# A DeltaNet and hard-swish MLP kernel on one core: X of steps 2 and 3 from products, the first steps in a new order, and products of the identity on TensorE

## The chip, the core and the metric

The kernel runs on one core of one Trainium2 chip. A core has TensorE (matrix products, PE in the profile; its weight loads are PEld), VectorE (DVE), ScalarE (ACT), GpSimd (POOL) and SyncE (SP), which here only issues DMAs. Each engine works through its own instructions in order; semaphores tie them together. TensorE's products land in PSUM, everything else lives in SBUF. The metric is the time of one execution on the device in microseconds; lower is better.

## The reference

Two computations follow each other. The first is a delta rule over 768 tokens, for 4 batches and 8 heads, head size 48:

```python
for t in range(S):
    y[:, :, t] = q_t @ state
    v_old = state^T k_t
    state = state + beta_t * outer(k_t, v_t - v_old)
```

with k normalised to length 1 first. Its output, 3072 tokens by 384, is x of the second:

```python
h = x @ w_in                         # 384 x 2048
g = h * clip(h + 3, 0, 6) / 6
out = g @ w_out                      # 2048 x 384
```

The arrays q, k, v and beta come in float32, the two weights in float64.

## The kernel before

**Steps.** The 768 tokens are cut into 24 steps of 32 tokens; a step holds the four batches beside each other in the 128 partitions. Within a step the sequential rule is a triangular system, so each step needs X, minus the inverse of a 32x32 unit triangular matrix for each head and batch. What is carried from step to step is `state`.

**Preparation of a step** (`prep`, L378 to L455). GpSimd normalises k into `kb` (L383), makes the masked beta `mb` (L391, two operations) and later `bkb` (L438); TensorE transposes k and q (`pt`, L409), ScalarE copies them out (`KQ`, L412), TensorE forms the score products (`sc`, L425), and VectorE multiplies them with `mb` into `LB` (L434). The norms come from `norms` (L337): square and sum (`sq`, `ss`), a square root on ScalarE, and small operations on VectorE.

**X in two ways.** For steps 0 and 1, `product` (L457) gets X by products of 32x32 blocks: six groups of products on TensorE (`pi`, L485), each followed by transposes and additions on VectorE or copies on ScalarE (L495 to L543), in strict alternation. For later steps, `inverse` (L551) takes a group of four steps at once: the matrices go out to DRAM and come back with one system to a partition (`A`), 30 rounds of a multiplication and a subtraction on VectorE solve them (L566, L571), and X goes out to DRAM and back into `LB`. The groups before are steps 0 and 1, then fours (2 to 5, 6 to 9, ...), and a last two.

**The chain of a step** (`chain`, L601): `ks` on TensorE from `state` (L622), `R` and `y` on VectorE (L635), `pz` (L643) with X, `Z` on ScalarE (L685), `su` (L710) and `py` on TensorE, the new `state` on VectorE (L726), and `yt`, the transposed output (L699), which feeds the MLP.

**The MLP** takes blocks of two steps. `up` (L750): 16 units of three products `ph` (L760), each with an activation on ScalarE (L765) and one operation `g` on VectorE (L772). `down` (L788) has plain products for the first two blocks (`po`, L795); from the third on `down_by_seven` (L836) uses seven half-size products (L856) with additions on VectorE.

**Weights.** Each of 16 pieces of 768 KB of float64 is loaded raw; `scales` (L288) builds its power of two in five activations of ScalarE, `convert` (L306) makes the float32 value in three operations of VectorE.

**What sets the order.** [...] The string `ORDER` (L22) lists by hand which generator advances next, until the chain of step 5 is done: `p` preparation, `x` product, `i` inverse, `h` chain, `n` norms, `a` scales, `c` convert, `u` one MLP unit, `g` its late VectorE part, and `k`, `q`, `v`, `w` loads. From step 6 on a loop with a fixed plan does it (L1043), 15 MLP units to a step. Loads go to SP's queue; some of the first k and q loads, and the DMAs of the first inverse, go to ScalarE's queue.

Of the kernel before, what the change touches and what calls it, by code (L numbers as in the profile page):

```python
# [22 lines left out]
n0*8 n1 p0 n1 p0 n1 p0 q*2 p0 q p1 q p1 n1 p0 p1 a n1 a*2 p0 q*2 a*2 c a q p1 x0 n1*2 a n1*3 a  # L23
p2*2 x0 q c k2 p2 a p1 p3 x1 c p3*2 p2 a x1*2 p2 p4 p1 a*2 x1 k2*2 p3 p2 a*3 p3 k2 p5 x0 c*2
k2*3 p3 x0 c a*4 x0 k2 c*3 p4 p5 k2*2 x1 k2 x0 p4 c*2 p5 p4 p5 p4*2 p5 x1*2 k2 x0 p5 a x1 a i1 c
x0 x1 a x0 c x1 k2 x1 x0*2 k2 c i1 v k2 i1 x1 i1 x0 i1*2 a i1*2 x0 q i1*3 a i1 h0*2 i1*3 q i1*3
h0 i1*3 v i1 x1 i1 q i1 h0 i1*3 a i1*2 a h1 a*2 h1 i1*2 h0 i1 h1 q h1 i1 c i1 v h1*2 v i1 h1 k2
i1*5 v i1 v i1 v c w v i1 a c a*2 i1 a i1 c i1 v q i1 a v*2 i1 v a c i1*4 w i1*2 h1 n2 i1*4 a
i1*3 a i1 h2 i1*2 c a i1 a i1 n2 a c*2 u a g c n2 a c u a n2 g u n2*3 a n2 q c a g n2*2 a c a p6
h2 u h2 c p6 a w p6 u q*2 a v g q*2 a h2 p6 c q*2 v u p7 a q p6 a q p7 p6 v p8 c g q h2 v h2 a c  # L30
w a p7 a k3 h3 u k3 p8 u a h2*2 k3 c g k3 g c h3 c h3 p8 a u k3 a k3 p7 u g q p8 u q w k3 p7 h3
a p9 p8 c a p9 k4 g p9 k4 p7 a*2 g u k3 k4 c k4 h3 a h3 p9 c w k3 k4 k3 a p9 g*2 h3 a c h4 k4 k3
u a h3 c g k4 h4 k3 c w u p8 k3*2 g k3 h4 k3 q a n3 a c n3 c a n3 u q u g u h4 a g p9 a c k4 h4
c a n3 a u a w k4 i2 w*2 a*2 u n3 a h4 v h5 h4 c a u c g n3 c n3*2 g v*2 u h4 n3 u v n3 u c p10
q a*2 q g k4 v q i2 p11 k4 u k4*4 p10 i2*2 q*2 i2*2 k4 u v i2*2 h5 v g h5 i2 a i2 q i2 p10 u h5
u v i2*2 q u i2*2 c i2 p10 g u i2 p10 i2*4 p11 p10 h5*2 q u q h5 p11 g u p11 i2 u i2*2 p12 i2 g
i2*2 p11*2 u i2*2 u i2*3 g i2 u*2 g i2 u*2 g u g u*2 g u i2*6 u*4 h5
# [4 lines left out]
def kernel(  # L42
# [34 lines left out]
    CB = 2  # L77
    TB = CB * P
    assert N % CB == 0 and CB <= GS

# [6 lines left out]
    NPC, NPM = 2, 4  # L87
    psC = ctx.enter_context(tc.tile_pool(name="psC", bufs=NPC, space=PSUM))
    psM = ctx.enter_context(tc.tile_pool(name="psM", bufs=NPM, space=PSUM))
# [43 lines left out]
    def load_k(t, eng=nc.sync):  # L133

        g, i = group(t)
        if i == 0:
            needs(*(("kb", first(g - 2) + j) for j in range(size(g - 2) if g >= 2 else 0)))
            kfs[g] = stage.tile([P, GS, H, D], FP32, name="kf", bufs=2)
        for b in range(B):
            eng.dma_start(out=kfs[g][rows(b), i], in_=tokens(k, b, t))  # L140
            if b == B - 1:
                past.add(("k", t))
            yield

    def load_q(t, eng=nc.sync):
        if t < N:
            if t >= NQB:
                needs(("qT", t - NQB))
            for b in range(B):
                eng.dma_start(out=qbufs[t % NQB][rows(b), :, 0:D], in_=tokens(q, b, t))  # L150
                if b == B - 1:
                    past.add(("q", t))
                yield
# [3 lines left out]
    def load_v(t):  # L157
        if t < N:
            if t >= NVF:
                needs(("R", t - NVF))  # L160
            vfs[t] = stage.tile([P, H, D], FP32, name="vf", bufs=NVF)
            for b in range(B):
                nc.sync.dma_start(out=vfs[t][rows(b)], in_=tokens(v, b, t))
                if b == B - 1:
                    past.add(("v", t))
                yield
# [61 lines left out]
    places = const.tile([128, 6], FP32, name="places")  # L228
    for i, value in enumerate((1152 - 7.5 / 16, -1600.0, -448.0, -704.0, 704.0 * 128, 1e-30)):
        nc.vector.memset(places[:, i : i + 1], value)  # L230
    powers = (
        (ACTF.Relu, 1.0 / 16), (ACTF.Abs, 1.0), (ACTF.Relu, 1.0), (ACTF.Abs, 1.0),
        (ACTF.Relu, -128.0),
    )
# [53 lines left out]
    def scales():  # L288

        for i in range(NW):  # L290
# [5 lines left out]
            d, z = raws[i], like(es[i % 2], i)  # L296
            for n, (func, scale) in enumerate(powers):
                nc.scalar.activation(  # L298
                    out=z, in_=z if n else d.bitcast(I16)[:, :, :, 3], func=func,
                    bias=places[:, n : n + 1], scale=scale,  # L300
                )
                if n == len(powers) - 1:
                    past.add(("scale", i))
                yield
# [32 lines left out]
    def norms(g, i0, n):  # L337
# [17 lines left out]
        nc.scalar.activation(out=root[:], in_=ss[:], func=ACTF.Sqrt, bias=places[:, 5:6])  # L355
# [14 lines left out]
        for i in range(n):  # L370
            invs[first(g) + i0 + i] = inv[:, i, :]
        yield
# [5 lines left out]
    def prep(t, dma):  # L378
# [3 lines left out]
        needs(*([("bkb", t - NKB)] if t >= NKB else []))  # L382
        nc.gpsimd.tensor_tensor(  # L383
# [17 lines left out]
        for j, src in enumerate((kb, qb)):  # L401
# [3 lines left out]
            ring("pm", NPM, ("pt", t, j))  # L405
            read(("pt", t, j))
            pt = psM.tile([128, NP, P], FP32, name="pt", tag="pm")
# [38 lines left out]
        if g > 0:  # L446
# [3 lines left out]
            dma.dma_start(  # L450
# [6 lines left out]
    def product(t, pool):  # L457
# [6 lines left out]
        needs(("bkb", t))  # L464
# [3 lines left out]
        VY = pool.tile([P, 2, H * C], FP32, name="VY", bufs=CB)  # L468
        V, Y = VY[:, 0, :], VY[:, 1, :]
        T = pool.tile([P, H * C], FP32, name="VT", bufs=CB)  # L470
        F = pool.tile([P, H * C], FP32, name="F", bufs=CB)
# [3 lines left out]
        def times(rhs):  # L475
# [3 lines left out]
            ring("pm", NPM, key)  # L479
            keys.append(key)  # L480
            ps = psM.tile([P, 2, H * C], FP32, name="pi", tag="pm")
# [69 lines left out]
    def inverse(g, dma, back):  # L551
# [5 lines left out]
        dma.dma_start(  # L557
# [4 lines left out]
        for j in range(1, C - 1):  # L562
# [3 lines left out]
            nc.vector.tensor_tensor(  # L566
# [4 lines left out]
            nc.vector.tensor_tensor(  # L571
# [3 lines left out]
        nc.vector.memset(A.rearrange("p c i -> p (c i)")[:, 0 : C * C : C + 1], -1.0)  # L575
        back.dma_start(
# [4 lines left out]
        for i in range(size(g)):  # L581
            yield
            LBv = LBs[first(g) + i][:].rearrange("p e a j w -> p (e a) j w")
            back.dma_start(out=LBv[:, :, 0, :], in_=x_dram[g][i].rearrange("h p c -> p h c"))
# [16 lines left out]
    def chain(t):  # L601
# [78 lines left out]
        ring("pm", NPM, ("pz", t))  # L680
        read(("pz", t))
        pz = psM.tile([P, 512], FP32, name="pz", tag="pm")
# [6 lines left out]
        def seam():  # L689

            blk, cc = divmod(t, CB)
# [3 lines left out]
            ring("pm", NPM, ("yt", t))  # L695
            read(("yt", t))
            pt = psM.tile([128, NKT, P], FP32, name="yt", tag="pm")
# [21 lines left out]
        ring("pm", NPM, ("py", t))  # L719
        py = psM.tile([P, 512], FP32, name="py", tag="pm")  # L720
# [29 lines left out]
    def up(blk):  # L750

        needs(*(("seam", blk * CB + i) for i in range(CB)))
        xT = xTs[blk]
        for f in range(NFC):
            needs(("w", f * 128 // WP))
            settle(2)
            ring("pm", NPM, ("ph", blk, f))
            ph = psM.tile([128, TB], FP32, name="ph", tag="pm")
# [23 lines left out]
    def to_dram(t, o):  # L782
        for b in range(B):
            r0 = b * S + t * C
            eng = nc.scalar if t >= N - CB and b % 2 else nc.sync
            eng.dma_start(out=out[r0 : r0 + C, :], in_=o[rows(b ^ 1)])

    def down(blk, c, f0):  # L788

        needs(("w", NWI + f0 // WF))  # L790
        if f0 == 0:
            ring("pm", NPM, ("po", blk, c))
            pos[c] = psM.tile([128, DM], FP32, name="po", tag="pm")
# [5 lines left out]
        if f0 + WF == NFC:  # L799
            if c == 0:  # L800
                pos["o"] = mlp[0].tile([128, CB, DM], FP32, name="o", bufs=1)
# [3 lines left out]
            to_dram(blk * CB + c, o)  # L805
# [14 lines left out]
    assert 2 * WP * NKT == HF * HM and CB == 2 and HF % 2 == 0  # L820
# [15 lines left out]
    def down_by_seven(blk):  # L836
# [8 lines left out]
        o = mlp[0].tile([128, CB, DM], FP32, name="o", bufs=1)  # L845
        u = mlp[0].tile([128, HM], FP32, name="u", bufs=1)[:]
        C11, C12, C21, C22 = (o[:, c, m : m + HM] for c in range(CB) for m in (0, HM))
        ps = {}

        def product(n, a, b, half):  # L850

            if half == 0:
                ring("pm", NPM, ("po", blk, "by", n))
                ps[n] = psM.tile([128, HM], FP32, name="po", tag="pm")
# [60 lines left out]
        to_dram(blk * CB + 1, o[:, 1])  # L915
        product(3, A12, B22, 1)
        add(C12, u, ps[3][:])
        to_dram(blk * CB, o[:, 0])
        yield

    def mlp_units():
# [4 lines left out]
        for f in range(0, NFC, WF):  # L926
            for c in range(CB):
# [6 lines left out]
        for blk in range(1, N // CB):  # L934
            if blk < FIRST:
                settle()
                for c in range(CB):
# [5 lines left out]
            if blk + 1 < N // CB:  # L943
# [21 lines left out]
    LA = CB + GS  # L965
# [6 lines left out]

    def prep_of(t):
        return made(("p", t), lambda: prep(t, nc.scalar if t < LA else nc.sync), t < N)

# [3 lines left out]
    def norms_of(g):  # L979
        return made(("n", g), lambda: norms(g, 0, size(g)), g < NG)  # L980

    def inverse_of(g):
        return made(("i", g), lambda: inverse(g, nc.scalar if g == 1 else nc.sync, nc.sync), g < NG)

    def keys_of(g):
        return made(
            ("k", g), lambda: chained(*(load_k(first(g) + i) for i in range(size(g)))), g < NG
        )

    def pieces(i):  # L990
        for i in range(i, NW):
            load_w(i)
# [5 lines left out]
    gens["w"] = pieces(NWI)  # L998

    with tc.manual_schedule():  # L1000
        with tc.tile_pool(name="early", bufs=2) as early:
            for t in range(LA):
                drain(load_k(t, nc.scalar if t % 2 else nc.sync))
                if t == 1:
                    drain(load_q(0))
                    drain(load_q(1, nc.scalar))
            for t in range(CB, NQB):
                drain(load_q(t))
            for i in range(3):
                load_w(i, early if i < 2 else stage)  # L1010
            for t in range(CB):
                drain(load_v(t))
# [99 lines left out]
```

## Time and profile before

| | us |
|---|---|
| median of 3 runs | 724.28 (723.74 to 726.2) |
| the profiled execution's own time | 726.81 |
| its span, first to last instruction | 725.1 |
| TensorE busy | 656.7 (91%) |
| VectorE busy | 454.9 (63%) |
| ScalarE busy | 247.3 (34%) |
| GpSimd busy | 89.5 (12%) |

The profile page cuts the span into 40 slices of 18.1 us; a digit is the busy share of an engine in tenths. PEclk is the clock granted to TensorE, in tenths of full speed. In the answers by window, the columns are the window, its length, and for PE, PEld, DVE, ACT and POOL the busy time and the number of instructions; then the clock, the share of the DMA engines and GB/s. In the timeline a line is start, duration, engine, line of the program and tile; the bracket is the idle time before it and what ended that. In the groups, after the bar, come busy time and the mean of one in ns, then idle time before the group.

A product in float32 is two records in the trace.

### The profile page before, as it was taken

To read this page: it belongs to the slowest core of one execution; us is meant where nothing else is said; L and a number is where in the kernel's file an instruction comes from. 1 tells how busy PE (TensorE), PEld (TensorE's weight loads), DVE (VectorE), ACT (ScalarE), POOL (GpSimd) and SP (SyncE) were. 2 spreads that over 40 slices of the span, in tenths; PEclk is the share of its full clock that TensorE was granted. 3 is DMA by queue.
4 is the path that set the end of the run, shared out by engine and by line. 5 is a ranking of instruction groups with operands and counts; after the bars stand their busy time and mean duration, and the time that the engine had idled before them with its cause. 6 is when DMAs were issued, how large, how long until landed. Compare 5 with 4: busy or idle time off the path is not lost.

```text
span 725.1 us, 25019 instructions
## 1 busy us (share of the span) xinstructions
PE 656.7 (91%) x10984; PEld 571.9 (79%) x10984; DVE 454.9 (63%) x1209; ACT 247.3 (34%) x467; POOL 89.5 (12%) x128
## 2 busy tenths in 40 slices
PE   0666839798979999999999999999999999999997
PEld 0455627666756789889889899898898898989997
DVE  6556996488583379665489464598444894533343
ACT  1763688593130331331322322322313213222130
POOL 3640024004031101041110031000000000000000
PEclk9966569899999999999999999999999999999999
DMA  7954437472042312421410411212302001000000
GB/s 135 298 119 89 112 91 176 90 183 37 8 96 48 75 32 42 90 36 26 96 32 15 98 33 31 52 21 60 53 2 50 13 16 39 2 24 1 23 1 22
DMA packets 135853, 44.72 MB, mean 62 GB/s; under 512 B 126112, under 2 KB 129184, under 8 KB 135744
## 3 DMA queue, kind: packets, MB, share of 16 engines
q1 hardware_dynamic: 126832, 40.99, 25.4%
q10 hardware_dynamic: 8912, 2.13, 1.5%
q8 instruction: 86, 1.41, 0.8%
q14 instruction: 23, 0.19, 0.1%
HBM read 32.60 MB, written 10.49 MB: 59 GB/s over the span
## 4 chain that ended last, share of the span: by engine, by line
PE 78%; issue 7%; DVE 5%; DMA 4%; POOL 2%; ACT 2%; SPq 1%; POOLq 0%; DVEq 0%
PE ph L760 31%; PE po L856 26%; PE po L795 3%; PE pz L643 3%; PE ks L622 3%; PE su L710 3%; PE py L643 3%; PE pt L409 3%; PE sc L425 2%; DMA kf<-in_k_dram 2%; DMA spare<-in_moe_w_in_dram 1%; PE pi L485 1%; ACT spare L298 1%; DMA vf<-in_v_dram 1%; PE yt L699 1%
## 5 line engine op out<-in xcount | busy, mean ns | idle before, releaser
L760 PE MATMUL ph<-xT,w_in 128*128 128x256 f32 x1152 | 269.6, 386 | 2.6 <-issue 2.3
L760 PEld LDWEIGHTS ph<-xT,w_in 128*128 128x128 f32 x1152 | 216.4, 193 | 34.7 <-issue 3.0
L765 ACT ACTIVATE t<-ph,halves 128x256 f32<-128x256 f32 x192 | 90.8, 474 | 207.3 <-PE ph L760 204.6
L772 DVE SCALAR_TENSOR_TENSOR g<-t,ph 128x256 f32<-128x256 f32 x192 | 79.8, 418 | 120.5 <-ACT t L765 120.3
L856 PE MATMUL po<-w_out,g 128*128 128x192 f32 x640 | 111.9, 327 | 0.0
L856 PEld LDWEIGHTS po<-w_out,g 128*128 128x128 f32 x640 | 104.2, 190 | 0.5
L856 PE MATMUL po<-spare,g 128*128 128x192 f32 x480 | 87.2, 330 | 0.0
L856 PEld LDWEIGHTS po<-spare,g 128*128 128x128 f32 x480 | 78.0, 190 | 1.2
L298 ACT ACTIVATE spare<-spare,places 128x768 uint16<-128x768 uint16 (+1 forms) x74 | 69.2, 940 | 7.7 <-DVE w_in L327 3.3
L566 DVE TENSOR_TENSOR pr<-A 128x30 f32<-128x30 f32 (+19 forms) x180 | 62.8, 349 | 4.1
L571 DVE TENSOR_TENSOR A<-A,pr 128x30 f32<-128x30 f32 (+19 forms) x180 | 61.9, 344 | 4.1
L842 DVE TENSOR_TENSOR g<-g 128x256 f32<-128x256 f32 x160 | 60.4, 428 | 3.7 <-PE po L856 3.5
L409 PE MATMUL pt<-ident,kb 128*128 128x128 f32 x96 | 18.3, 326 | 32.8 <-POOL kb L383 32.8
L795 PE MATMUL po<-w_out,g 128*128 128x384 f32 x128 | 45.4, 494 | 0.0
L383 POOL TENSOR_TENSOR kb<-kf,inv 128x384 f32<-128x384 f32 x24 | 23.5, 979 | 176.0 <-DVE inv L369 73.0
L412 ACT ACTIVATE KQ<-pt 128x512 f32<-128x512 f32 x48 | 28.2, 594 | 47.4 <-PE pt L409 47.4
L409 PEld LDWEIGHTS pt<-ident,kb 128*128 128x128 f32 x96 | 13.8, 167 | 36.0 <-POOL kb L383 33.8
L863 ACT ACTIVATE o<-po 128x192 f32<-128x192 f32 x40 | 13.2, 331 | 82.8 <-PE po L856 79.7
L391 POOL TENSOR_TENSOR mb<-beta_tok,mask 128x256 f32<-128x256 f32 x48 | 33.8, 724 | 56.2 <-DVE LB L434 56.2
L726 DVE TENSOR_TENSOR state<-state,su 128x384 f32<-128x384 f32 x46 | 23.3, 548 | 22.2 <-PE su L710 22.2
L795 PEld LDWEIGHTS po<-w_out,g 128*128 128x128 f32 x128 | 23.5, 192 | 12.9 <-issue 0.5
L635 DVE SCALAR_TENSOR_TENSOR R<-ks,parity,vf 128x192 f32<-128x192 f32 x46 | 16.9, 410 | 26.3 <-PE ks L622 26.2
(97 smaller groups left out, 581.5 us busy)
## 6 DMA issues: line engine op xcount, KB each, us to landing
spare<-in_moe_w_out_dram SPq DMA_DIRECT2D x8, 768.0 KB, 5.4
vf<-in_v_dram SPq DMA_DIRECT2D x96, 48.0 KB, 2.6
qb<-in_q_dram SPq DMA_DIRECT2D x92, 48.0 KB, 2.4
out_dram<-o SPq DMA_DIRECT2D x92, 48.0 KB, 1.6
kf<-in_k_dram SPq DMA_DIRECT2D x84, 48.0 KB, 2.8
w_out<-in_moe_w_in_dram SPq DMA_DIRECT2D x4, 768.0 KB, 9.6
LB<-x_dram SPq DMA_DIRECT2D x22, 128.0 KB, 3.1
x_dram<-A SPq DMA_DIRECT2D x5, 512.0 KB, 2.8
```

Source lines behind the costliest of these rows:

```text
L298: nc.scalar.activation(out=z, in_=z if n else d.bitcast(I16)[:, :, :, 3], func=func, bias=places[:, n : n + 1], scale=scale,)
L391: nc.gpsimd.tensor_tensor(out=mb[:, e], in0=beta_tok[:, t, e:H:2].unsqueeze(2).unsqueeze(3).to_broadcast([P, NP, 2, C]), in1=mask2[:].unsq ...
L409: nc.tensor.transpose(pt[:, p, :], src[:, 2 * p : 2 * p + 2].rearrange("p e w -> p (e w)"), ident[:])
L566: nc.vector.tensor_tensor(out=pv, in0=A[:, j, j + 1 :].unsqueeze(1).to_broadcast([n, j, w]), in1=A[:, 0:j, j].unsqueeze(2).to_broadcast([n ...
L571: nc.vector.tensor_tensor(out=A[:, 0:j, j + 1 :], in0=A[:, 0:j, j + 1 :], in1=pv, op=ALU.subtract)
L643: nc.tensor.matmul(ps[rows(place(b)), D * h : D * h + D], lhsT=m(h)[rows(b)], rhs=z[rows(b), D * h : D * h + D], start=True, stop=True, sk ...
L760: nc.tensor.matmul(ph[:], lhsT=w_in[:, s, f * 128 : (f + 1) * 128], rhs=xT[:, s, :], start=(s == 0), stop=(s == NKT - 1),)
L765: nc.scalar.activation(out=t1[:], in_=ph[:], func=ACTF.Relu, bias=half, scale=1.0 / 6.0)
L772: nc.vector.scalar_tensor_tensor(out=g, in0=t1[:], scalar=1.0, in1=ph[:], op0=ALU.min, op1=ALU.mult)
L795: nc.tensor.matmul(pos[c][:], lhsT=gs[blk, f // 2][:, f % 2, c * P : (c + 1) * P], rhs=w_out[:, f, :], start=(f == 0), stop=(f == NFC - 1),)
L842: nc.vector.tensor_tensor(out=A(f, *out), in0=A(f, *a), in1=A(f, *b), op=op)
L856: nc.tensor.matmul(ps[n][:], lhsT=A(f - f % 2, *a)[:, f % 2], rhs=b[:, f], start=(f == 0), stop=(f == HF - 1),)
```

## The change

- **Groups.** Steps 0 to 3 now form the first group (`CB` 4; a new `BK` = 2 keeps the MLP's blocks). X of steps 2 and 3 also comes from `product`; the buffers are shared with steps 0 and 1, so step 2 follows step 0 and step 3 step 1. The groups with an inverse are 4 to 7, 8 to 11, up to 20 to 23: five in place of six.
- **The first inverse** (steps 4 to 7) runs on GpSimd; the others stay on VectorE.
- **Identity products.** `busy` multiplies the identity with itself into a PSUM tile that nothing reads. The word `z` puts one into TensorE's order; there are 79, all before the first MLP unit.
- **PSUM.** Until the first MLP unit there are three buffers and one for the identity products, after it four as before.
- **Scales** take three activations in place of five.
- **Norms** of steps 0 and 1 are made each by itself, and `kb` of step 0 on VectorE.
- **Loads** of k, q, v and weights are all placed by the new `ORDER`. A word in capitals uses ScalarE's queue: two k loads and two q loads. The DMAs of the first inverse go to SP's queue.
- **ORDER** is new as a whole. Before its first `u` stand the preparations of steps 0 to 7 (before: 0 to 5), products 0 to 3 (before: 0 and 1 and all of the first inverse), the chains of steps 0 and 1 and the beginning of step 2, and 20 `c` words (before: 22). Both versions have 46 `u` words in it, and the same loop afterwards.

```diff
 ORDER = """
-n0*8 n1 p0 n1 p0 n1 p0 q*2 p0 q p1 q p1 n1 p0 p1 a n1 a*2 p0 q*2 a*2 c a q p1 x0 n1*2 a n1*3 a
...
+q K0 k0 q Q q k0 K0 w Q k0 q k0 m0 k0*2 m0*3 q m0 m1*7 q a m0*2 a p1 p0 c a k1 k0 q*2 c p1 c k1
+q k0*2 q k0 q k0*2 p1 p0 k0 p1 p0 p1 z*3 p0 k1 x1 p1 k1*3 q p0 x1 k1 k0 q w q*2 w n0 x0 p0 z*10
+x0 x1 k1 q n0 z*2 x1 k1 x0 k1 x1 z*2 x0 n0*2 a c x1 x0 a k1 x0 x1 k1 a k1 v*2 n0 x1 x0 v a x0 x1
+n0 k1 c x1 k1 x0 k1 w n1*2 q n1 v z*2 x0 n1 v*2 w a n1*2 v n1 v w n1*3 v w*2 a q*2 x0 q*2 z*28
...
-    CB = 2
-    TB = CB * P
+    CB, BK = 4, 2
+    TB = BK * P
...
-    powers = (
-        (ACTF.Relu, 1.0 / 16), (ACTF.Abs, 1.0), (ACTF.Relu, 1.0), (ACTF.Abs, 1.0),
-        (ACTF.Relu, -128.0),
-    )
...
+            nc.scalar.activation(
+                out=z, in_=d.bitcast(I16)[:, :, :, 3], func=ACTF.Relu,
+                bias=places[:, 0:1], scale=1.0 / 16,
+            )
+            yield
+            nc.scalar.activation(
+                out=w, in_=z, func=ACTF.Prelu, bias=places[:, 1:2], scale=-1.0, alpha=TINY
+            )
+            yield
+            nc.scalar.activation(
+                out=z, in_=w, func=ACTF.Prelu, bias=places[:, 2:3], scale=-128.0 / TINY, alpha=TINY
+            )
...
-        nc.gpsimd.tensor_tensor(
+        (nc.vector if t == 0 else nc.gpsimd).tensor_tensor(
             out=kb[:, :, 0:D], in0=kfs[g][:, i],
...
-        needs(("bkb", t))
+        needs(("bkb", t), *([("X", t - 2)] if t >= 2 else []))
...
-    def inverse(g, dma, back):
+    def inverse(g, eng):
...
-            nc.vector.tensor_tensor(
+            eng.tensor_tensor(
                 out=pv, in0=A[:, j, j + 1 :].unsqueeze(1).to_broadcast([n, j, w]),
                 in1=A[:, 0:j, j].unsqueeze(2).to_broadcast([n, j, w]), op=ALU.mult,
             )
...
+    def busy():
+
+        nc.tensor.matmul(
+            idle[0][:], lhsT=ident[:], rhs=ident[:], start=True, stop=True,
+            skip_group_check=True,
+        )
...
-        return made(("i", g), lambda: inverse(g, nc.scalar if g == 1 else nc.sync, nc.sync), g < NG)
+        return made(("i", g), lambda: inverse(g, nc.gpsimd if g == 1 else nc.vector), g < NG)
...
+                queue[0] = nc.scalar if word[0].isupper() else nc.sync
+                word = word.lower()
+                if word == "z":
+                    busy()
+                elif word == "g":
...
+        NPM[0] = 4
+        psM[0] = ctx.enter_context(tc.tile_pool(name="psM", bufs=NPM[0], space=PSUM))
```

## The prediction

> **What bounds the kernel now.** I read the 40 slices first, then windows cut where the slices change, then the order of TensorE's instructions, then the costliest groups.
>
> ```profile
> PE   0666839798979999999999999999999999999997
> ...
> PEclk9966569899999999999999999999999999999999
> ```
>
> TensorE is full from slice 12 on; gaps and the low clock lie before it. The windows give that in numbers:
>
> ```profile
> 16.00:36.00 20.00, 13.23 (x346) 10.61 (x346) 12.82 (x25) 13.59 (x19) 13.41 (x16) 1.00 0.93 285
> 36.00:88.00 52.00, 34.73 (x1373) 29.98 (x1374) 37.87 (x87) 28.80 (x40) 7.31 (x8) 0.62 0.49 113
> 88.00:106.00 18.00, 5.69 (x24) 4.57 (x23) 17.32 (x45) 13.27 (x19) 1.07 (x1) 0.69 0.27 61
> 106.00:204.00 98.00, 89.53 (x1624) 68.85 (x1624) 67.28 (x148) 55.12 (x92) 21.62 (x28) 0.93 0.43 97
> ...
> 217.00:725.00 508.00, 504.21 (x7462) 450.75 (x7446) 299.63 (x832) 131.21 (x289) 35.67 (x46) 1.00 0.18 37
> ```
>
> After 217 us TensorE sets the end (504 of 508 us, full clock), VectorE is busy 59%. Before 88 us nobody is full: VectorE 73%, TensorE 67% at clock 0.62. In TensorE's timeline four instants cut the run:
>
> ```profile
> 87.60 6.09 PE L760 MATMUL ph<-xT,w_in 128*128 128x256 f32 x24
> 106.25 1.11 PE L409 MATMUL pt<-ident,kb 128*128 128x128 f32 x4 [12.56 <-POOL kb L383]
> ...
> 204.01 1.15 PE L622 MATMUL ks<-state,KQ 64*64 64x48 f32 x64
> ...
> 215.32 1.50 PE L643 MATMUL pz<-R,LB 32*32 32x48 f32 x64 [3.36 <-DVE g L772]
> ```
>
> The MLP's first product runs at F = 87.6; then TensorE waits 12.6 us for GpSimd's `kb`, late because its norms lie behind the inverse on VectorE; step 6 begins (its `ks`) at 204.0; it then waits 3.4 us for X. From step 6's `ks` on, the changed program issues exactly the same TensorE instructions. So the change is worth what it moves that instant, and the wait after it.
>
> Prices of the work that moves:
>
> ```profile
> L566 DVE TENSOR_TENSOR pr<-A 128x30 f32<-128x30 f32 (+19 forms) x180 | 62.8, 349 | 4.1
> L571 DVE TENSOR_TENSOR A<-A,pr 128x30 f32<-128x30 f32 (+19 forms) x180 | 61.9, 344 | 4.1
> ...
> L383 POOL TENSOR_TENSOR kb<-kf,inv 128x384 f32<-128x384 f32 x24 | 23.5, 979 | 176.0 <-DVE inv L369 73.0
> ...
> L391 POOL TENSOR_TENSOR mb<-beta_tok,mask 128x256 f32<-128x256 f32 x48 | 33.8, 724 | 56.2 <-DVE LB L434 56.2
> ```
>
> One inverse costs VectorE (62.8 + 61.9)/6 = 20.8 us.
>
> **The Trainium skill.** "TensorE: Matmul & The Clock Gate", Part 1, says that an idle window of some 3.4 us halves the clock and a busy one restores it. The trace agrees on the first (0.50 at 96 to 104, after a gap), on the second only for large products: at 72 to 76 us TensorE was busy 3.87 of 4 us with small tiles at 0.50, and the `ph` products brought it to 0.88, then 0.97. "GPSIMD Engine Reference", section 3.1, puts a two-input elementwise operation there at 1.96 times VectorE's; here 384 elements take 0.83 to 0.98 us against 0.56 to 0.61, so 1.5 to 1.7. Its section 8 says that GpSimd shares SBUF interfaces with VectorE: at 44 us two `bkb` took 3.04 us instead of 1.64, and L322 on VectorE 1.25 instead of 0.94.
>
> **The change, part by part.**
>
> *Until F.* It adds X of steps 2 and 3 by products: per product VectorE issues 13 operations of 0.38 to 0.5 us (the rows of L493 to L543), 5.6 us; TensorE four groups at 0.8 and two at 1.0 warm (0.9 and 1.9 cold, from 36 to 66 us), 5.2 warm, 7.4 cold. It moves the preparation of steps 6 and 7 ahead of F, and takes the inverse of steps 2 to 5 off VectorE (20.8 us). Start: in the kernel before, ScalarE issued 8 k loads from 8.9 to 13.7 us and only then the square root; now 4 loads stand there, norms of steps 0 and 1 go one by one, `kb` of step 0 is VectorE's. Loads issue in 0.58 us, the last of step 0 at 5.5, landing 2.5 later, step 1's at about 11 behind a weight: sq and ss 1.1, root 0.3, small operations 1.6, so `kb` at 14 instead of 15.3. From there VectorE has to issue before the first `g`: 4 products 22.6, 8 LB 5.5, six sq and ss 6.7, small norms 2.5, weight conversion 16.9 (7 at 0.55, 7 at 0.94, 6 at 1.07), steps 0 to 2's R, y and state 7.7: 62 us. At its 73% of before F = 14 + 85 = 99; full, 76. Two products run interleaved with six preparations, so I take 79%: F = 92. TensorE, as check: 8 preparations at 8 transposes of 0.11 and `sc` 0.79 (13.4), products 20.8, steps 0 to 2 8 us, 79 identity products: two passes of half a `ph` record, 0.215 each, 17: 59 us warm from 16 us, 75; all cold (transposes 0.22, `sc` 1.0, `py` 1.5, identity 0.43) some 100, so 116. Half and half 96. Both checks surround 92. That F is no earlier than before (87.6) buys two more X and two more preparations.
>
> *Conversion on ScalarE* goes from 80 to 48 operations of 0.94, 30 us less. I cost it at nothing: ScalarE is busy 34%. Where the chain passes through it (46 to 50 and 57 us), about 4.7 us could come off; that is in the 78%.
>
> *Loads on SP's queue.* The k of steps 4 to 7 end as 48 loads of 0.58 and 3 weights of 0.5: 31 us, landed at 34. Their sq stand on VectorE before the fifth round of products 0 and 1, reached at 14 + 18/0.85 = 35. So nothing, but no slack; a later landing holds VectorE one for one. Behind them v of step 0 (33 us) is needed at 45. The k loads of group 2 wait on SP for `kb` of step 3, with v of step 2 behind: needed only after F.
>
> *F to step 6.* TensorE work at full clock, before: 90 `ph` at 0.43 (38.7), 32 `po` at 0.645 (20.6), 48 transposes 5.3, 6 `sc` 4.7, four steps' pz, su, py 9.8, 3 `ks` 3.2, yt 1.3: 83.6 in 116.4 us, so 32.8 were lost: 12.6 for `kb`, 8.6 in small waits, some 5 to the clock, the rest to prices. After: 32 transposes and 4 `sc`: 80.3. The `kb` wait is gone (steps 6 and 7 are ready at F). I take 18 lost: small waits 9, clock 3, prices 5, X of step 4 1.
>
> *The inverse on GpSimd*, 60 dependent operations, 9,920 elements. No row shows them. From below: undisturbed `mb` (256) 0.59 and `kb` (384) 0.83 give 0.11 + 1.875 ns an element: 25 us. From above: each as dear as a mean `kb`, 59. I take 25 times 1.2 for contention, 0.1 for each wait on itself, 3.4 for step 8's operations in between: 40. The load of A lands at F + 8 (two `up` units, then 5.0), X goes out and back in 6: X of step 4 at F + 54. TensorE asks for it after 45.5 us of work and some 10 of stalls: F + 55. Just hidden; from 41 us on, every microsecond counts. Behind its `pz` stand steps 4 and 5, and the second MLP block.
>
> *After step 6's `ks`.* Before 725.1 - 204.0 = 521.1. X of step 6 is ready long before, so the 3.4 us wait and 1.3 of half clock behind it go: 516.4. One inverse fewer on VectorE (6 to 5) gives nothing, as TensorE is full.
>
> Sum: 92 + 80.3 + 18 + 516.4 = 706.7 of span. The profiled execution took 726.8 around its 725.1, while the median is 724.3, 0.8 under the span: so 706.
>
> **Rivals.** *The start runs smoothly*: the identity products hold the clock, VectorE works at 88%, F = 84, stalls 8: 84 + 80.3 + 8 + 516.4 - 0.8 = 688. For it: interleaved chains, and VectorE so full at 88 to 106 (17.3 of 18). Against: each round still goes TensorE, VectorE, TensorE, in order. *The identity products do not do what they are for*: the clock stays near 0.6 and 79 of them cost 0.43, F = 105: 719. For it: 72 to 88 us at 0.50 with TensorE full; against: `ph` lifted the clock in 4 us. *GpSimd becomes the bound (slower)*: if an operation costs nearly as much whatever its size, 60 at 0.98 and 3.4 are 62 us, X of step 4 is 21 us late: 727; with contention of 1.2 on top, 739. It decides from 0.95 us an operation. For it: 1.52 us per `bkb` seen; against: 256 elements are cheaper than 384 by a third.
>
> **How the numbers follow.** About 0.3% (2.2 us) is what a measurement of this kernel tells from no change. Forecast as summed: 0.55, own range 697 to 714 (F by 6, stalls by 6). Smooth start 0.15 (683 to 697). Cold clock 0.13 (714 to 722). GpSimd late 0.17, of which 0.05 ends within 0.3%, and 0.12 above. Faster 0.83, same 0.05, slower 0.12. For 8 in 10 I leave out half of the smooth start and the slower end: 690 to 722.
>
> **What would show it.** First `ph` at 86 to 98; clock 36 to F over 0.75; step 6's `ks` at 184 to 196 and 516 us after it; the GpSimd groups of the inverse at 0.4 to 0.65 us each; `pz` of step 4 waiting under 5 us. Wrong: a wait of `pz` or `Z` for LB's load above 10 us, VectorE waiting for k loads before F, or a stretch after step 6's `ks` that is no shorter than 521.

## The result and the profile after

The changed kernel takes 743.41 us (740.76 to 745.22), the kernel before, run beside it, 724.95: a ratio of 1.0252, 95% interval 1.0215 to 1.0288. It is slower; the forecast was 706. The profiled execution spans 741.8 us.

The slices of the page after (tenths of 18.5 us; the last line is the DMA queue that carries instructions, with packets, MB and its share):

```profile
PE   1768777995799999999999999999999999999997
...
PEclk9869898998999999999999999999999999999999
...
q8 instruction: 93, 1.52, 0.9%
```

TensorE now has work from slice 2 on, and its clock is high. Yet it is not full before slice 8. The windows after, with the columns of the windows shown of before:

```profile
16.00:36.00 20.00, 15.94 (x468) 14.27 (x471) 12.70 (x25) 7.65 (x12) 6.07 (x6) 0.88 0.69 153
36.00:54.00 18.00, 10.49 (x388) 9.42 (x378) 11.21 (x29) 2.73 (x5) 0.00 (x0) 0.65 1.00 260
54.00:72.00 18.00, 16.50 (x589) 14.74 (x589) 8.71 (x17) 5.72 (x11) 5.98 (x8) 1.00 0.30 74
72.00:90.00 18.00, 13.08 (x483) 11.25 (x482) 11.58 (x24) 5.52 (x10) 7.93 (x9) 0.81 0.33 77
90.00:118.80 28.80, 19.17 (x904) 16.39 (x892) 14.17 (x28) 11.47 (x17) 4.89 (x8) 0.96 0.34 64
118.80:225.00 106.20, 91.16 (x1511) 69.94 (x1513) 70.36 (x144) 50.81 (x87) 56.80 (x85) 0.93 0.37 88
225.00:741.80 516.80, 512.05 (x7618) 456.61 (x7618) 297.77 (x809) 134.30 (x295) 37.00 (x48) 1.00 0.19 39
```

Before 118.8 us no engine is full, and from 36 to 54 us all four idle a third of the time or more while the DMA engines are full. TensorE's timeline after (start, duration, what; in brackets the idle time before it and what ended that, "issue" being time in which the engine waited for nothing that the profile shows):

```profile
42.02 1.39 PE L499 MATMUL pi<-F,VT 32*32 32x32 f32 x87 [3.59 <-issue]
43.54 1.38 PE L499 MATMUL pi<-VY,VT 32*32 32x64 f32 x41
48.59 0.86 PE L499 MATMUL pi<-VY,VT 32*32 32x64 f32 x23 [3.68 <-issue]
...
52.17 6.52 PE L991 MATMUL idle<-ident 128*128 128x128 f32 x56
...
97.14 0.91 PE L499 MATMUL pi<-VY,VT 32*32 32x64 f32 x49 [2.00 <-issue]
97.98 0.49 PE L991 MATMUL idle<-ident 128*128 128x128 f32 x2
98.40 0.75 PE L499 MATMUL pi<-F,VT 32*32 32x32 f32 x64
99.01 0.31 PE L499 MATMUL pi<-VY,VT 32*32 32x32 f32 x12
101.13 0.65 PE L499 MATMUL pi<-VY,VT 32*32 32x32 f32 x52 [1.81 <-issue]
...
118.84 2.93 PE L774 MATMUL ph<-xT,w_in 128*128 128x256 f32 x6
...
173.47 1.12 PE L423 MATMUL pt<-ident,kb 128*128 128x128 f32 x4 [7.36 <-POOL kb L397]
...
181.35 0.88 PE L657 MATMUL pz<-R,LB 32*32 32x48 f32 x64
...
224.89 1.15 PE L636 MATMUL ks<-state,KQ 64*64 64x48 f32 x64
```

F is 118.84 (forecast 92, before 87.6). From F to step 6's `ks` it is 106.1 us (forecast 98.3, before 116.4), after it 516.9 (forecast 516.4, before 521.1). So most of what was lost against the forecast, 27 us, lies before F, and 8 us between F and step 6.

**What the pauses are.** Between 16 us and F TensorE pauses 15 times for "issue", 26.6 us in all, and waits about 1 us for other engines. A pause comes where a multiple of 128 product records is full: 87 + 41 between the pauses at 42.02 and 48.59, 49 + 2 + 64 + 12 = 127 between 97.14 and 101.13 (one record is missing). Each record has a weight load beside it, so this is 256 instructions; and one of the instruction queues (q8) moved 1.52 MB in 93 packets, 16.3 KB each. TensorE's 11,910 product records and 11,910 weight loads on the page are 93 times 256. This fits a page of the Trainium skill that I had not used: "Runtime: NRT & Kernel Launch", section "Instruction fetch mechanics", says that an engine's instructions come in blocks of 16 KiB, 256 instructions, by a DMA queue of its own. It adds that the cost of crossing into the next block is mostly hidden. Here it is not: from one pause to the next, 128 records take 3.6 to 4.2 us between 97 and 117 us, whatever is in them, and 6.6 us from 42.02 to 48.59. I read this as the pace at which TensorE gets its instructions.

The kernel before shows the same pace, in lines of its timeline that I had read over:

```profile
61.76 3.19 PE L485 MATMUL pi<-VY,VT 32*32 32x64 f32 x128 [0.91 <-issue]
65.60 0.97 PE L485 MATMUL pi<-VY,VT 32*32 32x32 f32 x91 [0.64 <-issue]
...
69.69 0.85 PE L643 MATMUL pz<-vf,LB 32*32 32x48 f32 x28 [0.55 <-issue]
```

3.84 us pass from 61.76 to 65.60, 4.09 to 69.69. But there TensorE had 1719 records from 14 us to F, or 13.4 blocks, 52 us at 3.9, in a stretch of 74 us in which it was idle for 26, 5 of them issue pauses. After, it has 2788 (identity products are 158 of them), 21.8 blocks, 85 us at 3.9. As an estimate, with the start at 16 us, F then comes at 101. This is no hard floor: at 3.4 us, the shortest block seen in any version, the same sum gives 90.

### The profile page after: what moved, and what is told of

It reads as the page before. It is cut to its first block, busy times and chain, and to the rows that moved or that the text cites. A ratio compares the mean times of both kernels' runs of the same rounds, so it can differ in the third digit from the quotient of the medians.

```text
span 741.8 us, 26810 instructions
## 1 busy us (share of the span) xinstructions
PE 678.4 (91%) x11910; PEld 592.6 (80%) x11910; DVE 436.3 (59%) x1119; ACT 222.3 (30%) x440; POOL 122.7 (17%) x186
## 3 DMA queue, kind: packets, MB, share of 16 engines
q8 instruction: 93, 1.52, 0.9%
## 4 chain that ended last, share of the span: by engine, by line
PE 85%; issue 4%; POOL 4%; SPq 2%; DMA 2%; DVE 2%; ACT 1%; POOLq 0%; DVEq 0%
PE ph L774 31%; PE po L870 25%; PE po L809 5%; PE ks L636 3%; PE pt L423 3%; PE pi L499 3%; PE py L657 3%; PE su L724 3%; PE sc L439 3%; PE idle L991 3%; PE pz L657 2%; POOL A L585 1%; SPq L146 1%; PE yt L713 1%; POOL pr L580 1%
## 5 line engine op out<-in xcount | busy, mean ns | idle before, releaser
L774 PE MATMUL ph<-xT,w_in 128*128 128x256 f32 x1152 | 266.7, 384 | 1.1 <-DVE g L786 0.9
L405 POOL TENSOR_TENSOR mb<-beta_tok,mask 128x256 f32<-128x256 f32 x48 | 35.9, 769 | 64.8 <-DVE LB L448 56.6
L397 POOL TENSOR_TENSOR kb<-kf,inv 128x384 f32<-128x384 f32 x23 | 20.6, 895 | 156.6 <-PE pt L423 92.6
L580 DVE TENSOR_TENSOR pr<-A 128x30 f32<-128x30 f32 (+14 forms) x120 | 43.0, 358 | 2.5
L585 DVE TENSOR_TENSOR A<-A,pr 128x30 f32<-128x30 f32 (+14 forms) x120 | 41.3, 344 | 2.7
L877 ACT ACTIVATE o<-po 128x192 f32<-128x192 f32 x40 | 13.2, 331 | 82.8 <-PE po L870 79.7
L499 PE MATMUL pi<-VY,VT 32*32 32x32 f32 (+1 forms) x1280 | 22.3, 224 | 15.8 <-issue 15.1
L499 PEld LDWEIGHTS pi<-VY,VT 32*32 32x32 f32 x1280 | 19.0, 122 | 19.1 <-issue 17.2
```

The lines of the kernel that those rows point to most:

```text
L405: nc.gpsimd.tensor_tensor(out=mb[:, e], in0=beta_tok[:, t, e:H:2].unsqueeze(2).unsqueeze(3).to_broadcast([P, NP, 2, C]), in1=mask2[:].unsq ...
L499: nc.tensor.matmul(ps[rows(b), 0:n, w], lhsT=T[rows(b), w], rhs=rhs[rows(b), :, w], start=True, stop=True, skip_group_check=True, tile_pos ...
L580: eng.tensor_tensor(out=pv, in0=A[:, j, j + 1 :].unsqueeze(1).to_broadcast([n, j, w]), in1=A[:, 0:j, j].unsqueeze(2).to_broadcast([n, j, w ...
L585: eng.tensor_tensor(out=A[:, 0:j, j + 1 :], in0=A[:, 0:j, j + 1 :], in1=pv, op=ALU.subtract)
L774: nc.tensor.matmul(ph[:], lhsT=w_in[:, s, f * 128 : (f + 1) * 128], rhs=xT[:, s, :], start=(s == 0), stop=(s == NKT - 1),)
```

## The experiments

**No identity products.**

```diff
-p1 z*3 p0 ... x0 p0 z*10 ... q*2 x0 q*2 z*28 x0 x1 ...
+p1 p0 ... x0 p0 ... q*2 x0 q*2 x0 x1 ...
```

> The changed kernel without its 79 identity products; nothing else moved. First theory: they stand in the way and the clock they buy is worth little, because TensorE before the first ph is held by pauses of 1 to 4 us that come after every 128 matmul records (its instruction supply) and by waits on VectorE. Then the first ph comes 5 to 12 us earlier than 118.8, the 6.5 us of 28 identity products ahead of the last round of product 0 go, and the time is 731 to 738. Rival: they hold the clock, and without them it falls to about 0.6 before the first ph; 16 of the 64-record groups at 1.9 in place of 1.0 us and steps 0 to 2 at twice their price make the first ph later than 118.8 by 5 us or more, 748 or over.

Measured: 733.86 us, 1.0082 of before (1.0061 to 1.0102), 9.6 less than with them (12 by the two ratios to the kernel before). F is 107.97, 10.9 earlier, though the clock from 14 us to F falls from 0.88 to 0.81. They cost more than the clock they bought. From 16 us to F TensorE's busy time falls by 13.2 us (75.2 to 62.0) and its idle time rises by 2.3 (27.7 to 30.0), so it is above all their own work that goes; as instructions they are 1.2 blocks, 4.8 us at 3.9. There are still 20.8 us of issue pauses.

**Without the row of 28 alone.**

```diff
-... q*2 x0 q*2 z*28 x0 x1 n0 ...
+... q*2 x0 q*2 x0 x1 n0 ...
```

> The changed kernel without the one row of 28 identity products ahead of the last round of products 0 and 1; the other 51 stay. First theory: VectorE had the inputs of that round ready at 53.4 us, the row ran till 58.6, so pz of step 0 comes 4 to 5 us earlier than 59.98 and the first ph about as much, 738 or so. Rival (the row pays for itself through the clock): step 0 is earlier, but steps 0 and 1 and the products after it run at the low clock, and the first ph is no earlier than 118.

Measured: 743.9 us in a single execution, where the changed kernel has 740.76 to 745.22. `pz` of step 0 comes 4.6 us sooner (55.39), but F only 2.3 (116.50), and step 6's `ks` is where it was (225.11). A difference of 2.3 in F says nothing by itself, as the run after the next one shows.

**The first inverse on VectorE.**

```diff
-        return made(("i", g), lambda: inverse(g, nc.gpsimd if g == 1 else nc.vector), g < NG)
+        return made(("i", g), lambda: inverse(g, nc.vector), g < NG)
```

> The changed kernel with the inverse of steps 4 to 7 back on VectorE, at its place in the order. If GpSimd's queue is what holds step 9's kb and X of step 4 (53.8 us of inverse), the 7.4 us wait at 173 goes; but VectorE takes 20.8 us more between the first ph and step 6, where it is busy about two thirds. Theory: the wait moves from GpSimd to VectorE's g and LB operations and the stretch from the first ph to step 6's ks (106.1 us) changes by less than 6 us either way. Rival: VectorE has that room, and the stretch falls to 96 or less. The first ph stays at 118 to 119.

Measured: 744.19 us in a single execution, F 119.68, F to step 6's `ks` 105.6. In TensorE's timeline of this run the wait for `kb` has given way to others:

```profile
150.85 0.66 PE L423 MATMUL pt<-ident,kb 128*128 128x128 f32 x4 [2.10 <-POOL kb L397]
...
168.85 4.54 PE L809 MATMUL po<-w_out,g 128*128 128x384 f32 x8 [4.42 <-DVE w_out L340]
```

VectorE is now late with `w_out`, 4.42 us, and step 8's `kb` with 2.10: 6.5 in place of 7.4.

**Step 8's preparation and its q loads later.**

```diff
-k3 p8 a u g ... c p8 i1*2 ... i1 p8 i1 v ... i1 p8 v i1 ... u g q*2 i1 q n3 i1 q u g i1*2 p8 n3 v ... u i1 a i1 ... c i1 c a ... i1 a u
+k3 a u g ... c i1*2 ... i1*2 v ... i1 v i1 ... u g p8 i1 n3 p8 i1 u g i1 p8 i1 n3 v ... u i1 p8 a i1 ... c i1 p8 c a ... i1 a q*4 u
```

> The changed kernel with the preparation of step 8 (and four q loads behind it) later in the order, so that GpSimd does not stand 9.0 us inside the inverse waiting for the norms of group 2. Theory: the inverse ends about 9 us before 172.5, step 9's kb follows at about 164, TensorE's 7.4 us wait at 173 and the low clock behind it go, and the stretch from the first ph to step 6's ks falls from 106.1 to 96 to 99. Rival: another wait takes its place (X of step 4 through DRAM, weight conversion for the down products, or the chain of steps 4 and 5), and it stays above 103. First ph as before at 118 to 119.

Measured: 732.04 us in a single execution, 11.4 less than the changed kernel's median and 8.7 below its fastest. F to step 6's `ks` is 97.6, the wait for `kb` 1.89.

F itself came 3.2 us earlier, at 115.64. The edit cannot have done that: the two orders are the same up to the tenth `u`, behind F. So this is how far F lies apart between executions. With the same words before F it is 118.84, 119.68 (the inverse on VectorE) and 115.64 here; without identity products it is 107.97 in one version and 103.08 in the next. A difference in F of less than 5 us between two single profiles therefore shows nothing.

**Both: no identity products, step 8 later.**

> The changed kernel without identity products and with step 8's preparation later. If the two costs are separate, they add: first ph at 106 to 109, 97 to 99 us from there to step 6's ks, 516.9 after it, so a span of 722 to 725 and a time level with the kernel before. Rival: the clock is low at the first ph without identity products and the wait for step 9's kb comes back in another place; then 729 or more.

Measured: 725.77 us, 1.0005 of before (0.9981 to 1.0029). F is 103.08, F to step 6's `ks` 101.1 (107.7 with step 8 unmoved), the rest 516.8; the profiled execution (722.84) is the fastest of twelve. From its timeline:

```profile
38.83 0.91 PE L499 MATMUL pi<-F,VT 32*32 32x32 f32 x51 [1.57 <-issue]
...
52.34 0.26 PE L657 MATMUL pz<-vf,LB 32*32 32x48 f32 x1
...
85.70 1.17 PE L499 MATMUL pi<-VY,VT 32*32 32x64 f32 x34 [1.54 <-issue]
...
89.47 0.75 PE L499 MATMUL pi<-VY,VT 32*32 32x32 f32 x36 [0.93 <-issue]
...
103.08 2.93 PE L774 MATMUL ph<-xT,w_in 128*128 128x256 f32 x6 [1.12 <-DVE LB L557]
...
152.24 0.66 PE L423 MATMUL pt<-ident,kb 128*128 128x128 f32 x4 [3.60 <-POOL kb L397]
```

The block from 85.70 to 89.47 takes 3.77 us. TensorE has 2631 records up to F, 20.6 blocks, so at 3.9 F would be at 96. The clock from 14 us to F is 0.69 here and 0.81 with step 8 unmoved, where F, behind the same words, is 4.9 later: in these two executions the higher clock did not bring F nearer. In this profiled execution F comes 15.5 us later than before, the stretch from F to step 6's `ks` is 15.3 shorter and the rest 4.3; by the medians nothing is left. Of the 17.6 us between the medians of the changed kernel and this version, the identity products account for 9.6 and step 8's place for 8.1 (12 and 6 by the ratios). Without these two faults the change costs what it brings.

**Weights later (no identity products either).**

```diff
-q*2 w n0 ... v a x0 x1 ... x0 k1 w n1*2 ... v*2 w a n1*2 v n1 v w n1*3 v w*2 a q*2 ...
-x0 x1 n0 x1 x0 h0*2 n0 p3 c h0 q h0*2 v*2
+q*2 n0 ... v x0 x1 ... x0 k1 n1*2 ... v*2 n1*2 v n1 v n1*3 v q*2 ...
+x0 w x1 n0 x1 x0 w h0 w h0 n0 a p3 c h0 w a q h0 w a h0 w v*2
```

> The kernel without identity products, with the loads of weight pieces 2 to 7 (and the three ScalarE operations on piece 2) moved from between the rounds of products 0 and 1 to the chain of step 0. Theory: TensorE's pauses after every 128 matmul records are its instruction supply, which comes over the same DMA engines as the weights; with the DMA share at 36 to 54 us down from 1.00, the three pauses of 2.7, 4.0 and 4.0 us at 32 to 49 us become 0.5 to 2 each, and pz of step 0 comes 4 to 7 us before the 55.4 without this. Rival: the pauses are the supply's own latency and have nothing to do with the weights; they stay at 2.7 to 4 us, pz of step 0 stays within 1.5 us of 55.4.

Measured: 731.76 us in a single execution. TensorE's timeline of this run:

```profile
33.33 0.65 PE L499 MATMUL pi<-VY,VT 32*32 32x32 f32 x52 [1.01 <-issue]
...
36.76 0.91 PE L499 MATMUL pi<-F,VT 32*32 32x32 f32 x51 [1.31 <-issue]
...
40.76 1.71 PE L499 MATMUL pi<-VY,VT 32*32 32x64 f32 x53 [1.01 <-issue]
...
47.95 0.91 PE L499 MATMUL pi<-VY,VT 32*32 32x32 f32 x51 [1.37 <-issue]
...
55.14 1.16 PE L724 MATMUL su<-Z,bkb 32*64 32x48 f32 x55 [3.80 <-issue]
```

Without the move the pauses from 32 to 55 us are 2.66, 0.63, 4.04, 4.03 and 1.64 us; here the first ones are 0.46 (at 29.36) to 1.37, and `pz` of step 0 comes 6.8 us sooner, at 48.63 (3.7 sooner than in the version with both edits). Then the moved loads fill the DMA engines (share 1.04 and 1.06 from 45.7 to 54.7 us) and the pause of 3.80 stands there. F is 107.38, between the two values that the unmoved order gave.

**Four pieces of weights not loaded (no identity products either).**

```diff
-        nc.sync.dma_start(
+        if not NR <= i < NWI: nc.sync.dma_start(
             out=raws[i].rearrange("p s f z -> p s (f z)"), in_=src.bitcast(U32)
         )
...
+    for f in range(4): nc.gpsimd.memset(w_out[:, 4 * f : 4 * f + 4, :], 1.0)
```

> The changed kernel without identity products, and with four of its eight pieces of w_in (3 MB, loaded from 37 to 43 us) not loaded at all: their buffers are filled with ones at the start, so the output is not the reference's, but every engine has the same instructions before F as in no_identity. Theory (TensorE's issue pauses before F are long because its instructions are fetched over DMA engines that the weights fill, and F follows these pauses): the two pauses of 4.0 us at 42 and 49 fall to 0.4 to 1.5, pz of step 0 runs at 48 to 50 instead of 55.4, and as nothing is loaded later, most of that stays: F at 101 to 104 instead of 108.0. Rival (something else, as the low clock or VectorE's chains, sets the rest up to F): the pauses shrink, but F is at 106 to 108.

Measured: 728.71 us in a single execution (with all weights 730.37 to 734.9). F is 104.63 and `pz` of step 0 at 51.95, both some 3.4 us earlier than in the profile with all weights, between the two theories. TensorE's timeline:

```profile
41.68 0.91 PE L499 MATMUL pi<-F,VT 32*32 32x32 f32 x51 [4.31 <-issue]
...
45.68 1.70 PE L499 MATMUL pi<-VY,VT 32*32 32x64 f32 x53 [1.01 <-issue]
...
50.25 1.93 PE L499 MATMUL pi<-VY,VT 32*32 32x32 f32 x128 [2.87 <-DVE VY L552]
```

The pause of 4.03 at 49 fell to 1.01 and the next one went, with a DMA share of 0.35 from 41.7 to 45.7 us (1.09 with the loads). The pause at 42 stayed at 4.31, with a share of 0.89 before it from other loads: a piece of weights issued at 34.7, k and v. In the version with both edits it was 1.57, behind a share of 0.70. So the pauses are longest while loads fill the DMA engines, though not in step with the share. What the weights cost F is not shown: the version with both edits, with the same words before F and all weights, has `pz` at 52.34, and F at 103.08, earlier than here. The clock had fallen to 0.50 here, against 0.86 with all weights, in the window from 36 to 54 us.

**The identity products in quarters.**

```diff
-        nc.tensor.matmul(
-            idle[0][:], lhsT=ident[:], rhs=ident[:], start=True, stop=True,
...
+        for c in range(0, 128, 32):
+            nc.tensor.matmul(
+                idle[0][:, c : c + 32], lhsT=ident[:], rhs=ident[:, c : c + 32],
...
```

> The changed kernel with each identity product issued as four products of 32 columns: the same array work, 8 records in place of 2, 474 more. Theory of the instruction supply: 3.7 more blocks of 128 records have to come before the first ph, at 1 to 2 us each, so the first ph is 4 to 8 us later than in the changed kernel (115.6 to 119.7 over its relatives so far), and the row of 28 takes longer than 6.5 us. Rival: records cost nothing by themselves and only array time and waits do: the first ph stays at 115 to 120.

Measured: 821.65 us in a single execution, F 197.92. My assumption about their price was wrong: a record of a quarter takes 0.215 us where one of a whole takes 0.116. Two lines of TensorE's timeline and two windows of this run:

```profile
27.73 17.27 PE L992 MATMUL idle<-ident 128*128 128x32 f32 x80
...
68.28 48.00 PE L992 MATMUL idle<-ident 128*128 128x32 f32 x224
```

```profile
68.00:116.00 48.00, 48.00 (x240) 47.83 (x229) 1.88 (x7) 0.00 (x0) 0.00 (x0) 0.50 0.00 1
```

```profile
118.00:187.00 69.00, 69.00 (x1739) 65.22 (x1729) 29.27 (x58) 19.76 (x33) 19.00 (x24) 0.71 0.22 49
```

So it is no test of what I meant. But where 128 records last longer than 3.9 us, TensorE is never without instructions: from 118 to 187 us they last 5.1 us (69.0 / 1739 x 128), and it is busy throughout.

**The three scales alone, in the kernel before.**

```diff
-            for n, (func, scale) in enumerate(powers):
-                nc.scalar.activation(
...
+            nc.scalar.activation(
+                out=z, in_=d.bitcast(I16)[:, :, :, 3], func=ACTF.Relu,
+                bias=places[:, 0:1], scale=1.0 / 16,
+            )
...
```

> The kernel before with one part of the change alone: three activations in place of five for each weight piece, at the same places of the order. Theory: ScalarE is busy a third of the time and its shortfall lies on the chain only around 46 to 50 and 57 us, so the gain is 0 to 4 us: 720 to 727 beside the kernel before, same. Rival: the conversion of the weights is what the first MLP units wait for, and the shorter one brings the stretch from the first ph to step 6's ks down by more than 6 us.

Measured: 722.46 us, 0.9955 of before (0.994 to 0.997), the lowest median of all versions. F is 85.86 in place of 87.6, and F to step 6's `ks` 112.4 in place of 116.4.

**Earlier norms in that kernel** (the kernel before with the three scales), to see whether its wait for `kb` can be had as well.

```diff
-i1 c i1 v q i1 a v*2 i1 v a c i1*4 w i1*2 h1 n2 i1*4 a i1*3 a i1 h2 i1*2 c a i1 a i1 n2
+i1 c n2 i1 v q n2 i1 a v*2 n2 i1 v a c n2 i1 n2 i1 n2 i1 n2 i1 w n2 i1 n2 i1 h1 n2 i1*4 a i1*3 a i1 h2 i1*2 c a i1 a i1
```

> The kernel before with the three scales, and the norms of steps 6 to 9 (nine of their ten words) moved ahead of the last third of the inverse on VectorE; TensorE's order is the same. Theory (GpSimd's queue after F waits for norms that stand behind the inverse; that wait is worth its length only until the next thing is late, which is X of step 2): the wait of 11.5 us of the first transposes for kb at 104.5 falls under 2 us; the inverse, pushed back by 3.5 us of norms, lets X land at about 105 instead of 102, and pz of step 2, which runs at 109.0 now, waits for it 3 to 8 us and runs at 104 to 106: 718 to 720 us against 722.5. Rival (the wait moves whole, or the 3.5 us that VectorE spends earlier come back later): pz of step 2 at 108 to 110, 722 to 724 us.

Measured: 723.1 us, 0.9965 of before (0.9952 to 0.9979). A second version also has four words of conversion behind the inverse:

```diff
-i1 v q n2 i1 a v*2 n2 i1 v a c
+i1 q n2 i1 a n2 i1 a c
...
-c a i1 a i1 a
+c a v*2 i1 a v*2 i1 a
```

> The same, and the weight conversion on VectorE that stands between the norms and the end of the inverse (four words) moved behind the inverse. Theory (X of step 2 is next after kb): the inverse ends some 2 to 4 us sooner than in the run above, pz of step 2 runs at 100 to 103, 715 to 718 us. Rival (the first products of the MLP need those weights at once): the first ph groups wait for the conversion by as much, 718 us or more.

Measured: 724.29 us, 0.998 (0.9963 to 0.9997). In both the rivals' times came (none of the three versions is faster than the three scales alone), and what the first products of the MLP wait for (8.0 us in both) is `xT`: F is at 95.65 and 94.63. A third version puts the norms behind the word that issues `xT`:

```diff
-h1 n2 i1*4 a i1*3 a i1 h2 i1*2 c a i1 a i1 n2
+h1 n2*2 i1 n2 i1*2 n2 i1 a n2 i1*2 n2 i1 a n2 i1 h2 n2 i1 n2 i1 c a n2 i1 a i1
```

> As norms_earlier, but the nine words of the norms stand behind the word that issues the first MLP block's last xT, so that no xT on ScalarE waits behind a sq; TensorE's, GpSimd's and SP's orders are those of the kernel before with the three scales. Theory (in norms_earlier the wait of 11.5 us for kb did not go but moved to ScalarE's queue, where xT stood behind sq operations that waited for VectorE: 8.0 us): with F back at 84 to 87, kb is ready at 92 to 97 instead of 103 and the first transposes wait under 4 us; pz of step 2 then waits for X, which lands at about 105, and runs at 104 to 107 instead of 109: 718 to 721 us. Rival (VectorE, full at that place, sets the end whatever the order of its work: the inverse, the norms and the conversion are the same sum): pz of step 2 at 108.5 to 111, 722 to 724 us.

Measured: 723.32 us, 0.9966 (0.9952 to 0.9981). One line of TensorE's timeline from each: with the three scales alone, with the norms earlier, and with the norms behind `xT`:

```profile
104.50 1.12 PE L414 MATMUL pt<-ident,kb 128*128 128x128 f32 x4 [11.52 <-POOL kb L388]
```

```profile
95.65 7.51 PE L765 MATMUL ph<-xT,w_in 128*128 128x256 f32 x24 [7.99 <-ACT xT L705]
```

```profile
102.52 1.08 PE L414 MATMUL pt<-ident,kb 128*128 128x128 f32 x4 [8.33 <-DVE g L777]
```

The wait moves from `kb` to `xT` (which stood on ScalarE behind squares that waited for VectorE) and from there to `g`, but `pz` of step 2 runs at 108.96, 110.50 and 108.97. The rival of the third run fits: from 87 to 103 us VectorE is busy 14.4 of 16 us in it, and three orders of its work end alike. That work has to leave VectorE for this wait to go is the conclusion I draw; no run here shows it.

## Why the prediction was wrong, step by step

**"Until F" is the step that failed**: 92 forecast, 118.84 measured. VectorE's 62 us of work were right (60.2 from 14 us to F); its share of 79% (which the part on ScalarE calls 78%) was not (57%), because it waited for TensorE: 40.8 us of its listed waits in that stretch are for TensorE, 1.7 for ScalarE. TensorE's check, 16 us and then 59 us of work warm to 100 cold, was right in the work too (75.2 us busy), but it has no term for time in which TensorE has no instructions: 16 + 75.2 + 27.6 idle is F, and 26.6 of the 27.6 are issue pauses. "Both checks surround 92" compared two sums that lacked the same term. At 3.9 us for 128 records F comes at 101, or at 96 without identity products, by estimate. This number was to be had from the three lines of before above, and from counting the records that the change puts ahead of F: 1719 become 2788.

Of the 27 us, the runs place some 10 to 12 on the identity products (10.9 in F by two profiles, 9.6 by the medians, 12 by the ratios). The other 11 to 16 (F at 103.08 and at 107.97, with the same words before it) stand in executions with 17.5 and 20.8 us of issue pauses. That the pauses are these 11 to 16 us is read from the traces: no run took them away, and without them some of that time may go to waits for other engines. What keeps F above 96, and what the weights add, is not told apart.

**The identity products**: 0.215 us each was right, 56 records (28 products) took 6.52 us or 0.233 each, and so was a clock above 0.75 (0.87 from 36 us to F). Wrong was the tacit step that a higher clock brings F nearer: it came earlier at 0.81 without them, and earlier still at 0.69. If instructions set the pace, a faster TensorE only waits longer.

**F to step 6**: 98.3 forecast, 106.1 measured. TensorE was busy 91.2 us and idle 15.0; I had 80.3 of work, 8 for prices and clock, and 10 of waits. The waits are the larger part of the miss: `kb` of step 9 (7.36), of which I had said "The `kb` wait is gone", and an issue pause of 3.19 at 187.84 among the small products of step 4. GpSimd's timeline after shows why `kb` was late:

```profile
118.66 0.24 POOL L580 TENSOR_TENSOR pr<-A 128x30 f32<-128x30 f32 x1 [20.84 <-DMA A<-l_dram]
...
137.34 0.61 POOL L580 TENSOR_TENSOR pr<-A 128x240 f32<-128x240 f32 x1
146.96 0.83 POOL L397 TENSOR_TENSOR kb<-kf,inv 128x384 f32<-128x384 f32 x1 [9.00 <-DVE inv L382]
...
172.31 0.26 POOL L585 TENSOR_TENSOR A<-A,pr 128x30 f32<-128x30 f32 x1
...
172.58 0.84 POOL L397 TENSOR_TENSOR kb<-kf,inv 128x384 f32<-128x384 f32 x1
```

Step 8's `kb` stands in the middle of the inverse and waits 9.0 us for norms; `kb` of step 9 stands behind it. I counted 3.4 us for step 8's operations in between, but not what they wait for. Moving them gave 97.6, near the forecast's 98.3 partly by luck: TensorE was busy 90.2 there, 2 more than I had for work, prices and clock, and idle 2.6 less than my 10 of waits. Without identity products it gave 101.1.

**The inverse on GpSimd**: its price was right. The groups after:

```profile
L580 POOL TENSOR_TENSOR pr<-A 128x30 f32<-128x30 f32 (+14 forms) x30 | 17.1, 568 | 23.0 <-DMA A<-l_dram 20.8
L585 POOL TENSOR_TENSOR A<-A,pr 128x30 f32<-128x30 f32 (+14 forms) x30 | 19.0, 632 | 2.3
```

36.1 us, 0.60 each (forecast 0.4 to 0.65). With the 9.0 and step 8's operations it takes 53.8, but A landed at F - 0.2 and not at F + 8, and `pz` of step 4 (181.35) ran without a wait, as forecast. The rival "GpSimd becomes the bound" named the wrong cause for the right side: with step 8 later the price of the inverse stays and the wait for `kb` falls to 1.89.

**After step 6's `ks`**: 516.4 forecast, 516.9 measured, 516.8 to 517.4 in all versions of the changed order: right, with its reason.

**Small terms.** "`kb` at 14": it ran at 15.3 to 16.4, and the first transposes came 0.4 us earlier than before. Scales "at nothing": in the kernel before they bring 3.3 us (0.45%), so ScalarE's 34% hid less than I said. Why is not tested; VectorE and ScalarE alternate in one chain there. No load of k held VectorE, as forecast.

## What to carry to other kernels

Count instructions as well as work: where an engine gets many small ones, find the usual time between its issue pauses, and multiply by the number of blocks before anything is added to that stretch or put there to fill it. Before a few microseconds at one instant are read as an edit's doing, look at two executions in which nothing before that instant differs: here F was up to 4.9 us apart. A wait that ends on a full engine may be that engine's work under another name: three orders only moved the one for `kb`. And when an operation is put into the middle of a long one on an in-order engine, ask what it waits for, not only how long it lasts.

## What was not expected of the hardware

- From one issue pause to the next, TensorE never took less than 3.4 us for 128 product records with their weight loads: 3.4 to 4.2 in the shortest blocks of every version, in the kernel before too, and 6.4 to 7.2 where weights filled the DMA engines (a share of about 1.0); other values lie between. The large products of the MLP, 0.23 us a record (266.7 us / 1152), last 30 us a block; after step 6's `ks`, where they and the other large ones fill TensorE, the profile of the changed kernel lists no issue pause.
- A 128x128 float32 product record of the identity took 0.116 us with 128 columns (56 records in 6.52 us, clock 1.00). With 32 columns it took 0.216 us at a clock of 1.00 (80 records in 17.27 us) and 0.214 at 0.50 (224 in 48.00). Fewer columns made it dearer, and the clock made no difference.
- A busy TensorE did not bring the clock back with these products: from 68 to 116 us it was busy 48.00 of 48.00 us, and the granted clock stayed at 0.50.
- Dependent operations on GpSimd took 0.24 us for 30 elements and 0.62 for 240 a partition: by these two, a fixed part near 0.19 us and 1.8 ns an element (estimate).
